# A two-layer SSM and SwiGLU kernel: another hand-written order ahead of the first feed-forward group, the norms' mean factor on GpSimd, and a float32 inverse for three more pairs

## The chip, the cores and the metric

The kernel runs on one core of a Trainium2 chip. The metric is the device time of one execution in microseconds (us). The core's engines are TensorE (PE in the profile; its weight loads are PEld), VectorE (DVE), ScalarE (ACT), GpSimd (POOL) and SyncE (SP, which here only issues DMAs). Each engine works through its own instructions strictly in the order in which they stand in the program; a semaphore makes an instruction wait for another engine or for a DMA, and everything behind it on that engine waits too.

## What is computed

Four steps on x of 2048 rows by 512 columns, float32; the two kinds of step use the same weights both times.

```python
def _A_ref(u, ...):                       # SSM as a long convolution, one filter per column
    P = exp((dt * A)[:, :, None] * arange(L));  K = einsum("dn,dnl,dn->dl", C, P, dt * B).real
    y = irfft(rfft(u, 2L) * rfft(K, 2L))[:L] + u * Dskip
def _B_ref(x, w_gate, w_up, w_down):      # feed-forward, F = 1376
    return (silu(x @ w_gate) * (x @ w_up)) @ w_down
x = x + _A_ref(layernorm(x)); x = x + _B_ref(layernorm(x))
x = x + _A_ref(layernorm(x)); x = x + _B_ref(layernorm(x))
```

## The kernel before

The 2048 rows are worked in four blocks of T = 512. With two layers this makes eight (layer, block) pairs, in the order `SEQ = ((0,0),(0,1),(0,2),(1,0),(0,3),(1,1),(1,2),(1,3))`. The text counts them from 1 to 8, so the third to fifth pair are (0,2), (1,0) and (0,3). Each pair goes through `ssm` and then `ffn`.

**Before the first pair**, eight channel chunks of 64 columns are turned into filters: `lags` forms the filter's lags on TensorE (tiles `pk`), `spectra`, `first_parts` and `later_parts` transform them (`pw`, `wo`, `wos`, `w0r`), and the results go to DRAM (`wdr`). In the same stretch the feed-forward weights are cut into two float16 halves: `split(h, l, n)` issues `n` loads of float32 columns or rows into staging tiles, makes `h` high halves and `l` low halves. High halves come from ScalarE (line 675; the very first one from VectorE, line 673; lines 700 for w_down), low halves from VectorE (680, 703). The staging tiles share their space with other tiles, so a load waits until those are free.

**`ssm_half(layer, b, h)`** takes one half of the columns (256) of one pair. Its four steps multiply the pair's spectrum by filter spectra on VectorE: line 812 writes `yk` or `t`, line 815 adds `t` into `yk`, 820 and 821 form the complex result. Pair (layer, b) needs b + 1 such products a step, with `w` and `uu` loaded from DRAM on the SP queue. Lines 767, 768 and 833 to 845 combine four results into the four operands `v` of the inverse transform, which `inverse` runs on TensorE into `pi` (line 784). `inverse` has two forms. For pairs whose index in `SEQ` is at least `INV` it makes a float16 high part (`yl`, ScalarE, 776) and a low part (`yl`, VectorE, 232 through `stt`), and TensorE runs six float16 products of 256 columns; for the others TensorE takes `v` itself in float32, two products, each two records in the profile. `result` adds `pi` to the residual (`xg`, `xf`). The constants of the float16 form, `eih`, lie in the place of the float32 form's `ei`, so that their load (line 745) waits for the last float32 inverse.

**Norms.** `row_stats` serves all norms but the first three: ScalarE makes the row sums and the sums of squares (223, 225, 226), GpSimd takes the power -1/2 into `rs` (227), and VectorE multiplies mean and `rs` into `nb` (228), after which ScalarE applies both. It runs 21 times, 15 times for two row groups and six times for four.

**`ffn(layer, b)`** works on two halves of 256 rows. Six groups `pgu` of 48 float16 products (930, 931, 933; 899 to 901 for the remainder of 96 columns) hold gate and up in PSUM, of which two are held at a time. ScalarE applies Silu (936), VectorE multiplies with up (937), ScalarE and VectorE make the halves `hh` and `hl` (938, 939), and 946 to 948 multiply them by w_down into `py`. So the third group can start only when the first one's line 937 is done.

**What sets the order.** Up to the first feed-forward group the order is written out by hand: inside `tc.manual_schedule` each engine's instructions stand as the code issues them. There `conv[0]` and `conv[1]` are the two column halves of the first pair's `ssm`, `tail["sp"]` is what is left of a chunk's `spectra`, `odd` and `rest` are `later_parts` of the last two chunks, `last` is one forward transform of the second block, `norm` the first feed-forward norm and `block1` the second pair's `ssm`; `take(x, n)` issues the next n pieces of x. Behind that section the compile step's scheduler merges what is issued; instructions under `tc.high_priority` go first.

Of the kernel before, what the change touches and what calls it, by code (L numbers as in the profile page):

```python
# [16 lines left out]
OP = mybir.AluOpType  # L17
# [58 lines left out]
def kernel(ctx, tc, x, a_re, a_im, b_re, b_im, c_re, c_im, log_dt, d_skip,  # L76
# [139 lines left out]
    def row_stats(src, rows, scale, tag, junk):  # L216

        mv = tl([P, 4, 2], "mv", tag)
        rs = tl([P, 8], "rs", tag)
        nb = rs[:, 4:]  # L220
        c = 1.0 / (math.sqrt(D) * scale)
        for r in range(rows):
            A.activation(junk(r), src[:, r], AF.Identity, scale=-c / D, accum_out=mv[:, r, 0:1])
        for r in range(rows):
            A.activation(junk(r), src[:, r], AF.Square, scale=c, bias=mv[:, r, 0:1], accum_out=mv[:, r, 1:2])
        A.activation(mv[:, :rows, 1], mv[:, :rows, 1], AF.Identity, bias=epst[:, 0:1] if scale == 1.0 else epst[:, 1:2])  # L226
        G.tensor_tensor(rs[:, :rows], mv[:, :rows, 1], mhalf[:, :rows], OP.pow)  # L227
        V.scalar_tensor_tensor(nb[:, :rows], mv[:, :rows, 0], 1.0 / c, rs[:, :rows], OP.mult, OP.mult)
        return rs, nb

    def stt(o, i0, s, i1, op1):
# [281 lines left out]
    def skip(ch, kt, eng):  # L513

        k = kt[0:1, :, 0]
        eng.tensor_tensor(k, k, dsk[:, ch * DC:(ch + 1) * DC].rearrange("p (g d) -> p g d", g=4), OP.add)
# [97 lines left out]
    def sizes(ch, kt, junk):  # L614

        A.activation(junk, kt, AF.Abs, accum_out=wsum[:, ch:ch + 1])
# [36 lines left out]
    def split_weights():  # L653
# [5 lines left out]
        def columns(j, wi, src):  # L659
            fs = slice(j * cb, (j + 1) * cb)  # L660
            sc = sc6[:, wi:wi + 1]
            at = []

            def load():
                tag = next(tags)
                st = tl([P, 4, cb], "st2", tag) if isinstance(tag, str) else \
                    wsl[3].bitcast(F32)[:, 4 * cb * tag:4 * cb * (tag + 1)].rearrange("p (k f) -> p k f", k=4)
                nc.sync.dma_start(st, src[:, fs].rearrange("(k p) f -> p k f", p=P))
                at.append(st)

            def hi():
                if j == 0 and wi == 0:
                    V.tensor_scalar(wgu(wi, 0, 0, 4)[:, :, fs], at[0], sc, None, OP.mult)
                else:
                    A.activation(wgu(wi, 0, 0, 4)[:, :, fs], at[0], AF.Copy, scale=sc)

            def lo():
                n = 2 if wi == 0 else 4
                for k in range(0, 4, n):
                    V.scalar_tensor_tensor(wgu(wi, k, 1, n)[:, :, fs], at[0][:, k:k + n], sc,  # L680
                                           wgu(wi, 0, 0, 4)[:, k:k + n, fs], OP.mult, OP.subtract)
            return load, hi, lo
# [292 lines left out]
    with tc.manual_schedule(engines={mybir.EngineType.Activation, mybir.EngineType.DVE, mybir.EngineType.PE, mybir.EngineType.Pool}):  # L975
# [228 lines left out]
        split(1, 0)  # L1204
        first_parts(c, 0)
        take(conv[0], 1)
        split(1, 1)
        split(0, 0, 1)
        first_parts(c, 2)
        split(1, 0)  # L1210
        take(conv[0], 1)
        first_parts(c - 1, 1)
        split(1, 0)
        take(last, 2)
        take(conv[1], 1)
        first_parts(c - 1, 3)
        take(conv[1], 1)
        split(0, 1)
        split(0, 0, 1)
        take(conv[0], 1)  # L1220
        take(conv[1], 1)
        split(1, 1)
        split(0, 0, 1)
        take(conv[1], 1)
        split(0, 1)
        split(0, 0, 1)
        take(odd, 2)
        take(conv[1], 1)
        direct_size()
        block1 = ssm(0, 1)  # L1230
        take(norm, 1)
        take(rest, 2)
        take(odd, 1)
        take(odd, 2)
        take(norm, 1)
        take(block1, 1)
        take(rest, 1)
        split(1, 0)
        take(odd, 1)
        take(norm, 1)  # L1240
        split(0, 1)
        take(rest, 3)
        take(conv[0], 1)
        take(conv[1], 1)
        ready = nhl2[:, 0, 0], nhl2[:, 0, 1]
        split(1, 1)
        take(rest, 3)
        split(1, 1)
        take(rest, 4)
        split(0, 0, 3)  # L1250
        sizes(c, kts[1], ks)
        nn2 = tl([P, 2, D], "nn2", "nn")
    small[0] = itertools.repeat("sml")
    pscale = product_scale()
# [52 lines left out]
```

## Time and profile before

| | |
|---|---|
| median of three runs | 1091.86 us (1090.23 to 1092.86) |
| the profiled execution | 1091.58 us, span 1089.4 us |
| TensorE busy | 1026.5 us, 94% of the span |
| VectorE busy | 969.3 us, 89% |
| ScalarE busy | 547.4 us, 50% |
| GpSimd busy | 109.6 us, 10% |
| first product of a feed-forward group | at 300.5 us |

The profile's stretches, rows by line and waits below are all from that one execution, in us from its start. "Busy" is time in which at least one of an engine's instructions ran; two neighbours on an engine overlap a little at their ends, so the distance from one start to the next is somewhat less than an instruction's duration, and on TensorE much less. A releaser behind "<-" names what ended a wait.

### The profile page before, as it was taken

The page shows a single profiled execution, that of the slowest core. Times are in us where ns is not written, and L with a number is a line of the kernel's source. Part 1 is how long each engine was busy: PE and PEld are TensorE (multiplying, and loading weights), DVE is VectorE, ACT ScalarE, POOL GpSimd, SP SyncE. Part 2 cuts the span into 40 slices and gives each one's busy share as a digit, 9 for nine tenths or more (in the row PEclk, how much of TensorE's full clock was granted, in tenths as well). Part 3 has the DMA queues.
Part 4 walks back from the last instruction along what each step waited for, and adds up shares of the span by engine and source line. Part 5 has one row for each costly group of instructions (what it writes and reads, how often), then busy time and mean ns, then how long its engine had stood idle before and what let it go on. Part 6 is the DMA issues. An engine that isn't in the chain of part 4 may idle for free.

```text
span 1089.4 us, 22811 instructions
## 1 busy us (share of the span) xinstructions
PE 1026.5 (94%) x9302; PEld 810.9 (74%) x9302; DVE 969.3 (89%) x1405; ACT 547.4 (50%) x1093; POOL 109.6 (10%) x163
## 2 busy tenths in 40 slices
PE   1989999998779999999999999999999999999998
PEld 1868888887677777686779676786867687686775
DVE  8999999998999999999999989999998999993221
ACT  6989998953367162466462253533425432134211
POOL 1112222220002010012010001201100000000000
PEclk9989999998989999999999999999999999999999
DMA  5366777768765356342444553443545245312000
GB/s 212 108 180 167 173 166 179 187 181 272 234 182 172 120 145 215 105 141 68 131 117 133 158 160 130 119 136 100 166 126 180 59 127 147 109 61 63 2 25 20
DMA packets 125003, 149.23 MB, mean 137 GB/s; under 512 B 50897, under 2 KB 75985, under 8 KB 124130
## 3 DMA queue, kind: packets, MB, share of 16 engines
q1 hardware_dynamic: 112994, 122.27, 36.8%
q0 software_dynamic: 11904, 25.50, 10.0%
q8 instruction: 73, 1.20, 0.5%
q14 instruction: 32, 0.26, 0.1%
HBM read 97.66 MB, written 33.82 MB: 121 GB/s over the span
## 4 chain that ended last, share of the span: by engine, by line
PE 27%; DVE 27%; issue 11%; DMA 5%; ACT 3%; POOL 1%; SPq 0%; DVEq 0%; POOLq 0%; ACTq 0%
PE pgu L930 5%; PE pgu L931 5%; PE pgu L933 5%; DVE t L812 4%; DVE yk L815 4%; PE py L948 3%; PE py L946 3%; PE py L947 3%; DVE yk L812 3%; PE pi L784 2%; DVE sg L937 2%; DVE hl L939 2%; DMA n<-xdr 1%; DVE yl L232 1%; DMA mix<-nn 1%
## 5 line engine op out<-in xcount | busy, mean ns | idle before, releaser
L930 PE MATMUL pgu<-mix,wsl 128*128 128x256 f16 x1280 | 298.6, 273 | 5.4 <-DVE sg L937 2.1
L931 PE MATMUL pgu<-mix,wsl 128*128 128x256 f16 x1280 | 298.4, 273 | 0.0
L933 PE MATMUL pgu<-mix,wsl 128*128 128x256 f16 x1280 | 194.8, 273 | 0.0
L931 PEld LDWEIGHTS <-wsl 128*128 128x128 f16 x1280 | 125.2, 98 | 22.5 <-issue 6.7
L933 PEld LDWEIGHTS <-wsl 128*128 128x128 f16 x1280 | 125.2, 98 | 18.4 <-issue 3.8
L930 PEld LDWEIGHTS <-wsl 128*128 128x128 f16 x1280 | 125.2, 98 | 16.4 <-issue 1.2
L946 PE MATMUL py<-wsl,hh 128*128 128x512 f16 (+1 forms) x352 | 134.2, 381 | 0.1
L948 PE MATMUL py<-wsl,hl 128*128 128x512 f16 (+1 forms) x352 | 133.5, 381 | 0.1
L947 PE MATMUL py<-wsl,hh 128*128 128x512 f16 x320 | 121.8, 381 | 0.0
L815 DVE TENSOR_TENSOR yk<-yk,t 128x1024 f32<-128x1024 f32 x96 | 116.9, 1218 | 0.5
L812 DVE TENSOR_TENSOR t<-uu,w 128x1024 f32<-128x1024 f32 x96 | 117.0, 1218 | 0.3
L938 ACT ACTIVATE hh<-sg 128x512 f16<-128x512 f32 x80 | 50.1, 627 | 114.0 <-DVE sg L937 114.0
L544 PE MATMUL pw<-kt,ek 128*128 128x256 f32 (+1 forms) x384 | 93.2, 381 | 0.0
L937 DVE SCALAR_TENSOR_TENSOR sg<-pgu,sc,sg 128x512 f32<-128x512 f32 x80 | 59.6, 745 | 37.7 <-ACT sg L936 37.6
L936 ACT ACTIVATE sg<-pgu,sc 128x512 f32<-128x512 f32 x80 | 54.2, 678 | 70.7 <-PE pgu L933 66.9
L544 PEld LDWEIGHTS pw<-kt,ek 128*128 128x128 f32 x384 | 74.8, 199 | 8.8
L939 DVE TENSOR_TENSOR hl<-sg,hh 128x512 f16<-128x512 f32 x80 | 54.8, 685 | 15.3 <-ACT hh L938 15.3
L227 POOL TENSOR_TENSOR rs<-mv,mhalf 128x2 f32<-128x2 f32 (+1 forms) x21 | 33.6, 1598 | 336.3 <-ACT mv L226 296.3
L509 PE MATMUL pk<-re,g 128*32 128x64 f32 x1024 | 65.0, 317 | 2.2 <-DMA g<-g 1.9
L948 PEld LDWEIGHTS <-hl 128*128 128x128 f16 (+1 forms) x352 | 34.4, 98 | 39.2 <-issue 0.8
L947 PEld LDWEIGHTS <-hh 128*128 128x128 f16 (+1 forms) x352 | 34.6, 98 | 38.4 <-issue 0.8
L510 PE MATMUL pk<-im,g 128*32 128x64 f32 x1024 | 63.1, 301 | 0.0
(265 smaller groups left out, 2010.1 us busy)
## 6 DMA issues: line engine op xcount, KB each, us to landing
uu<-udr SPq DMA_DIRECT2D x96, 256.0 KB, 3.0
w<-wdr SPq DMA_DIRECT2D x96, 256.0 KB, 2.8
g<-g POOLq DMA_DIRECT2D x6, 1024.0 KB, 9.2
udr<-fu POOLq DMA_DIRECT2D x22, 256.0 KB, 2.7
udr<-u SPq DMA_DIRECT2D x16, 256.0 KB, 3.3
n<-xdr SPq DMA_DIRECT2D x4, 1024.0 KB, 6.4
kdr<-ks SPq DMA_DIRECT2D x6, 512.0 KB, 2.9
kt<-kdr SPq DMA_DIRECT2D x24, 128.0 KB, 3.0
```

The source lines that it names most:

```text
L509: PE.matmul(o, lhsT=g[:, 0, :, d], rhs=re[:, 0:64, d], start=True, stop=False, tile_position=(0, 32 * grp))
L544: PE.matmul(pw[:, i], lhsT=e, rhs=kt[:, :, c + 4 * k0:4 * k1:4, :].rearrange("p g k d -> p k g d"), start=c == 0, stop=c == 3)
L812: V.tensor_tensor(t, uu.unsqueeze(2).to_broadcast([P, NQ, 2, 2, DC]), w.unsqueeze(3).to_broadcast([P, NQ, 2, 2, DC]), OP.mult)
L815: V.tensor_tensor(yk, yk, t, OP.add)
L930: PE.matmul(o, lhsT=wgu(wi, k, 0)[:, fs], rhs=nh[:, k], start=k == 0, stop=False)
L931: PE.matmul(o, lhsT=wgu(wi, k, 1)[:, fs], rhs=nh[:, k], start=False, stop=False)
L933: PE.matmul(o, lhsT=wgu(wi, k, 0)[:, fs], rhs=nlo[:, k], start=False, stop=k == 3)
L937: V.scalar_tensor_tensor(sg, pgu[:, 1], sc6[:, 4:5], sg, OP.mult, OP.mult)
L939: V.tensor_tensor(hl[:, f0:f0 + 2], sg, hh[:, f0:f0 + 2], OP.subtract)
L946: PE.matmul(py[r], lhsT=hh[:n, f, rc], rhs=wd(f, 0)[:n], start=f == 0, stop=False)
L947: PE.matmul(py[r], lhsT=hh[:n, f, rc], rhs=wd(f, 1)[:n], start=False, stop=False)
L948: PE.matmul(py[r], lhsT=hl[:n, f, rc], rhs=wd(f, 0)[:n], start=False, stop=f == FT - 1)
```

## The change

Three edits. `INV` goes from 2 to 5, so that the third to fifth pair take the float32 inverse. In `row_stats` the scale moves out of the sums and `nb` becomes one GpSimd multiplication. In the hand-written section many `take` and `split` calls stand in another order; one of them, `take(block1, 1)`, is gone, and the very first high half of the weights moves from VectorE to ScalarE.

```diff
-INV = 2
+INV = 5
...
-        c = 1.0 / (math.sqrt(D) * scale)
+        c = 1.0 / (D * scale ** 2)
...
-            A.activation(junk(r), src[:, r], AF.Identity, scale=-c / D, accum_out=mv[:, r, 0:1])
+            A.activation(junk(r), src[:, r], AF.Identity, scale=-1.0 / D, accum_out=mv[:, r, 0:1])
...
-            A.activation(junk(r), src[:, r], AF.Square, scale=c, bias=mv[:, r, 0:1], accum_out=mv[:, r, 1:2])
-        A.activation(mv[:, :rows, 1], mv[:, :rows, 1], AF.Identity, bias=epst[:, 0:1] if scale == 1.0 else epst[:, 1:2])
+            A.activation(junk(r), src[:, r], AF.Square, bias=mv[:, r, 0:1], accum_out=mv[:, r, 1:2])
+        A.activation(mv[:, :rows, 1], mv[:, :rows, 1], AF.Identity, scale=c,
+                     bias=epst[:, 0:1] if scale == 1.0 else epst[:, 1:2])
         G.tensor_tensor(rs[:, :rows], mv[:, :rows, 1], mhalf[:, :rows], OP.pow)
-        V.scalar_tensor_tensor(nb[:, :rows], mv[:, :rows, 0], 1.0 / c, rs[:, :rows], OP.mult, OP.mult)
+        G.tensor_tensor(nb[:, :rows], mv[:, :rows, 0], rs[:, :rows], OP.mult)
...
-                if j == 0 and wi == 0:
-                    V.tensor_scalar(wgu(wi, 0, 0, 4)[:, :, fs], at[0], sc, None, OP.mult)
-                else:
-                    A.activation(wgu(wi, 0, 0, 4)[:, :, fs], at[0], AF.Copy, scale=sc)
+                A.activation(wgu(wi, 0, 0, 4)[:, :, fs], at[0], AF.Copy, scale=sc)
...
         take(conv[0], 1)
-        take(tail["sp"], 2)
+        take(conv[0], 1)
         spread_pe(ks, kts[1])
         skip(c, kts[1], G)
+        take(tail["sp"], 2)
...
-        take(block1, 1)
...
```

What the new order means is seen in the instructions. The change shifts the line numbers: 812, 815, 871, 609, 703, 680, 833, 841, 232 and 784 of before are 810, 813, 869, 610, 701, 678, 831, 839, 233 and 782 in it.

The first place is VectorE behind the first feed-forward norm's mean factor (213), before:

```order
L213 SCALAR_TENSOR_TENSOR rs<-mv,rs 128x2
L609 TENSOR_TENSOR wos<-pw,wos 128x2x3x64
L812 TENSOR_TENSOR yk<-u,w0r 128x1024
L812 TENSOR_TENSOR t<-uu,w 128x1024
L815 TENSOR_TENSOR yk<-yk,t 128x1024
L703 SCALAR_TENSOR_TENSOR wsl_2663<-st_3002,sc_92,wsl_2663 128x512 x2
L820 TENSOR_TENSOR bb<-yk 128x256
L821 TENSOR_TENSOR bb<-yk 128x256
L812 TENSOR_TENSOR t<-uu,w 128x1024
L812 TENSOR_TENSOR yk<-u,w0r 128x1024
L815 TENSOR_TENSOR yk<-yk,t 128x1024
```

The same place in the change:

```order
L213 SCALAR_TENSOR_TENSOR rs<-mv,rs 128x2
L701 SCALAR_TENSOR_TENSOR wsl_2663<-st_2935,sc_92,wsl_2663 128x512 x2
L610 TENSOR_TENSOR wos<-pw,wos 128x2x3x64
L869 TENSOR_TENSOR mix<-pt,mix 128x1024
L678 SCALAR_TENSOR_TENSOR wsl_2661<-wsl_2664,sc_92,wsl_2661 128x2x344
L678 SCALAR_TENSOR_TENSOR wsl_2662<-wsl_2664,sc_92,wsl_2661 128x2x344
L610 TENSOR_TENSOR wos<-pw,wos 128x2x3x64
```

The second pair's products (812, 815, 820, 821 from `u`, `uu` and `w`) have left this place; the low half of the first norm's output (869) and the weights' low halves stand directly behind the norm. Counted from the first pair's first product to the first line 937, VectorE has 118 instructions before and 96 in the change: four `t`, four `yk` from `u`, three of 815, four each of 820 and 821, two of 767, one of 768 and the 673 are fewer, and one 623 (a scalar of the inverse's scale) is added.

The second place is the inverse of the third pair's first column half. On VectorE, before:

```order
L833 TENSOR_TENSOR bb<-bb,mix 128x512
L815 TENSOR_TENSOR yk<-yk,t 128x1024
L910 TENSOR_TENSOR sg_3034<-sg_3034 128x2x96
L836 TENSOR_TENSOR mix<-bb 128x256
L837 TENSOR_TENSOR mix<-bb 128x256
L841 TENSOR_TENSOR bb<-bb,mix 128x512
L232 SCALAR_TENSOR_TENSOR yl_4065<-bb,sy,yl_4065 128x512
```

and in the change:

```order
L831 TENSOR_TENSOR bb<-bb,mix 128x512
L937 TENSOR_TENSOR hl<-sg_3021,hh 128x512
L813 TENSOR_TENSOR yk<-yk,t 128x1024
L233 SCALAR_TENSOR_TENSOR z_3022<-n,z_3022 128x1024
L834 TENSOR_TENSOR mix<-bb 128x256
L835 TENSOR_TENSOR mix<-bb 128x256
L839 TENSOR_TENSOR bb<-bb,mix 128x512
```

The low part `yl` is gone there, with its partner on ScalarE. On TensorE the same inverses are, in the change, products straight from `bb`:

```order
L782 MATMUL pi<-bb,mix 128x256 x2
L944 LDWEIGHTS hh
L944 MATMUL py<-wsl_2663,hh 128x512
L782 MATMUL pi<-bb,mix 128x256 x2
L945 LDWEIGHTS hh
```

where before six rows of the form `pi<-yl_4065,mix` stood for each operand.

The third place is GpSimd. Each power is now followed by the factor (229):

```order
L228 TENSOR_TENSOR rs<-mv,mhalf 128x2
L229 TENSOR_TENSOR rs<-mv,rs 128x2
L228 TENSOR_TENSOR rs<-mv,mhalf 128x4
L229 TENSOR_TENSOR rs<-mv,rs 128x4
L904 MEMSET sg_3021 128x4x32 x2
L737 DMA udr_114<-fu 128x512 x2
```

Behind these on GpSimd's queue stand the stores of a block's spectra (737), as before. On the SP queue the load of `eih` (745 before) moves from the third pair's start to the sixth's.

More of the change, by code (lines that the diff above doesn't have):

```diff
@@ L1203 @@
         scales()
-        split(1, 0)
+        take(conv[0], 1)
         first_parts(c, 0)
-        take(conv[0], 1)
-        split(1, 1)
-        split(0, 0, 1)
         first_parts(c, 2)
         split(1, 0)
+        first_parts(c - 1, 1)
+        first_parts(c - 1, 3)
+        take(conv[1], 1)
         take(conv[0], 1)
-        first_parts(c - 1, 1)
+        take(conv[1], 1)
+        split(0, 1)
+        split(0, 0, 1)
+        take(conv[1], 1)
         split(1, 0)
@@ L1215 @@
         take(conv[1], 1)
-        first_parts(c - 1, 3)
+        split(1, 0)
         take(conv[1], 1)
+        take(norm, 1)
+        split(0, 0, 1)
+        take(odd, 2)
+        take(rest, 2)
+        take(norm, 1)
+        split(1, 0)
+        take(odd, 1)
+        take(norm, 1)
+        ready = nhl2[:, 0, 0], nhl2[:, 0, 1]
+        block1 = ssm(0, 1)
         split(0, 1)
         split(0, 0, 1)
[L1220 to L1224, printed above, removed]
+        take(rest, 1)
         split(0, 1)
```

26 lines of the change are left out of this document (10 added, 16 removed).

## The prediction, made before the changed kernel ran

> **What bounds the kernel now.** I read the page's head, then busy time by stretch, then what TensorE waited for, then single rows. Of the page:
>
> ```profile
> PE 1026.5 (94%) x9302; PEld 810.9 (74%) x9302; DVE 969.3 (89%) x1405; ACT 547.4 (50%) x1093; POOL 109.6 (10%) x163
> ```
>
> The stretches (start and end, length, then busy us and instructions of TensorE, its weight loads, VectorE, ScalarE, GpSimd; granted clock, DMA share, GB/s):
>
> ```profile
> 246.00:300.00 54.00, 44.95 (x469) 39.78 (x468) 48.74 (x85) 17.84 (x28) 1.89 (x2) 0.91 0.79 256
> 300.00:329.00 29.00, 20.97 (x147) 19.31 (x147) 27.94 (x38) 19.76 (x47) 0.00 (x0) 0.88 0.61 182
> 329.00:420.00 91.00, 91.00 (x765) 68.67 (x763) 89.79 (x145) 40.99 (x80) 15.35 (x15) 1.00 0.53 152
> 420.00:700.00 280.00, 272.00 (x2272) 209.11 (x2270) 270.46 (x404) 133.34 (x265) 21.87 (x28) 0.99 0.43 132
> 700.00:910.00 210.00, 205.51 (x1686) 153.85 (x1684) 200.37 (x292) 83.73 (x160) 15.28 (x21) 1.00 0.45 130
> 910.00:1089.00 179.00, 175.20 (x1465) 132.38 (x1461) 94.52 (x134) 46.54 (x82) 2.00 (x5) 1.00 0.18 54
> ```
>
> There are two regimes. Up to 329 us VectorE is nearly full (27.94 of 29) while TensorE is idle for 8 of 29. From 329 us on TensorE is full: 743.7 of 760 us. So the end is the time at which TensorE becomes dense, plus its work from there, plus its waits. The last column of numbers on VectorE, 94.52 of 179, says that VectorE finishes early and doesn't set the end.
>
> What TensorE waited for, from 256 to 329 us and from 329 us on (total, times, longest):
>
> ```profile
> PE pw L544 <- DVE wos L609: 7.4, 2, 5.7
> PE pi L784 <- DVE bb L833: 3.6, 1, 3.6
> ...
> PE pi L784 <- ACT yl L776: 5.8, 4, 2.0
> PE pf L277 <- ACT fbt L278: 2.5, 1, 2.5
> PE pgu L930 <- DVE sg L937: 2.1, 2, 1.6
> ```
>
> All waits in the early stretch end on VectorE, which has the second pair's products between those that TensorE needs. The longest later wait is the float16 inverse's for its high part.
>
> **Part 1, the order up to the first gate product.** Two groups of the first feed-forward half can run before line 937 of the first is done; the third is where TensorE becomes dense:
>
> ```profile
> 292.34 0.15 DVE L213 SCALAR_TENSOR_TENSOR rs<-mv,rs 128x2 f32<-128x2 f32 x1
> ...
> 327.95 0.75 DVE L937 SCALAR_TENSOR_TENSOR sg<-pgu,sc,sg 128x512 f32<-128x512 f32 x1
> ...
> 328.75 0.27 PE L930 MATMUL pgu<-mix,wsl 128*128 128x256 f16 x1 [1.90 <-DVE sy L623]
> ```
>
> By the order, TensorE has the same things behind it at that point before and after: both column halves of the first pair, all of `later_parts`, 96 products of the group. So whatever the first 937 gains, the end gains, as far as TensorE stays dense. VectorE's rows up to there:
>
> ```profile
> L680 DVE SCALAR_TENSOR_TENSOR wsl<-wsl,sc,wsl 128x1376 f16<-128x1376 f32 (+1 forms) x8 | 10.1, 1285 | 0.0
> L812 DVE TENSOR_TENSOR yk<-u,w0r 128x1024 f32<-128x1024 f32 x5 | 6.1, 1217 | 0.0
> L815 DVE TENSOR_TENSOR yk<-yk,t 128x1024 f32<-128x1024 f32 x4 | 4.9, 1222 | 0.1
> L820 DVE TENSOR_TENSOR bb<-yk 128x256 f32<-128x256 f32 x10 | 4.3, 425 | 0.3
> L680 DVE SCALAR_TENSOR_TENSOR wsl<-st,sc,wsl 128x688 f16<-128x688 f32 x4 | 3.5, 927 | 0.0
> L703 DVE SCALAR_TENSOR_TENSOR wsl<-st,sc,wsl 128x512 f16<-128x512 f32 x4 | 2.8, 746 | 0.9 <-ACT wsl L700 0.9
> L609 DVE TENSOR_TENSOR wos<-pw,wos 128x384 f32<-128x384 f32 x4 | 2.2, 552 | 1.0 <-ACT wos L608 1.0
> L572 DVE TENSOR_TENSOR wo<-pw,wo 128x768 f32<-128x768 f32 x1 | 1.0, 969 | 2.3 <-ACT w0r L568 2.3
> L673 DVE TENSOR_SCALAR wsl<-st,sc 128x1376 f16<-128x1376 f32 x1 | 0.9, 936 | 0.0
> ```
>
> Ahead of 213 the change takes away 673 (0.9), one wide 680 (1.6, from the first row less its four narrow ones), four narrow ones (3.7), and a reduction left out of the sum; it adds one `yk` (1.2). The wait of 2.3 at 572 goes, because a step of the first pair now stands ahead of it. That is 5.0 + 2.3, so 213 falls to about 285. From 213 to 937 the change has 28 instructions where before had 44: six narrow and three wide 680 (10.4), four 703 (3.0), six 609 (3.3), one `t` and one 815 (2.4), one 871 (taken as an 815, 1.2), two 793 and a reduction (2, estimate from the 703) and scalars, about 23. Without any wait the first 937 would stand at 308, 20 us earlier. It will wait, since the cover is gone: the w_down load can only start when the first pair's last inverse frees its place, and it took this long:
>
> ```profile
> 291.33 5.25 DMA st<-in_B_w_down_dram
> ```
>
> VectorE's 703 stands right behind 213 now and needs that load and ScalarE's high half (0.7 by the 703's like); ScalarE then has 869, a wide high half and four pieces of `wos` ahead of the first 609. I count 2.5 to 3 us of waiting at each of these two and 1 at the next wide low half and at the Silu, 7 in all: the first 937 at 315, a gain of 13. The bounds are 20 (no wait) and 8 (the waits nearly double).
>
> **Part 2, the inverse.** One inverse in float32 (four records) and in float16 (six), each with the instruction that follows:
>
> ```profile
> 332.68 1.03 PE L784 MATMUL pi<-mix 128*128 128x256 f32 x4
> 333.54 0.27 PE L930 MATMUL pgu<-mix,wsl 128*128 128x256 f16 x1
> ...
> 550.26 0.82 PE L784 MATMUL pi<-yl,mix 128*128 128x256 f16 x6
> 550.91 0.82 PE L277 MATMUL pf<-z,eh 128*128 128x256 f16 x6
> ```
>
> From start to start that is 0.86 against 0.65 us. Three pairs with eight inverses each are 24 × 0.21 = 5.0 us more work on the engine that is full, with nothing to hide it. What it takes away lies on the other two:
>
> ```profile
> L776 ACT ACTIVATE yl<-bb,sy 128x512 f16<-128x512 f32 x32 | 22.8, 716 | 24.5 <-DVE bb L833 12.2 <-PE pi L784 8.0 <-DVE bb L837 4.2
> L232 DVE SCALAR_TENSOR_TENSOR yl<-bb,sy,yl 128x512 f16<-128x512 f32 x32 | 23.8, 745 | 1.1 <-ACT yl L776 1.1
> ```
>
> That is 24 × 0.72 = 17 us of ScalarE and 24 × 0.75 = 18 us of VectorE. Neither is full where TensorE is dense at the end, so their busy time is worth nothing by itself; what counts is the wait of 5.8 us for `yl` quoted above. It can go to zero (the second pair's float32 inverses lie in 329 to 420, where TensorE is busy for 91.00 of 91) or come back as a wait for `bb`, as 3.6 did before 329. I take 5 of it as gone. The load of `eih` moves to the sixth pair, where it waits for the last float32 inverse as it did at the third; the filter loads queue behind it on SP for as long. I cost it at nothing, and cover is VectorE's loaded `w` and `uu`; if that is gone, one landing of some 3 us.
>
> **Part 3, the mean factor.** VectorE loses the first of these rows, GpSimd gains one of its own:
>
> ```profile
> L228 DVE SCALAR_TENSOR_TENSOR rs<-mv,rs 128x2 f32<-128x2 f32 (+1 forms) x21 | 3.3, 157 | 10.4 <-POOL rs L227 10.4
> L227 POOL TENSOR_TENSOR rs<-mv,mhalf 128x2 f32<-128x2 f32 (+1 forms) x21 | 33.6, 1598 | 336.3 <-ACT mv L226 296.3 <-DVE sg L937 31.7 <-DMA uu<-udr 8.2
> L516 DVE TENSOR_TENSOR kt<-kt,tdk x7: 204/206/207, 73.0 to 239.0; 1x64 f32<-1x64 f32 x7
> L516 POOL TENSOR_TENSOR kt<-kt,tdk x1: 553/553/553, 261.3 to 261.3; 1x64 f32<-1x64 f32 x1
> ```
>
> VectorE is rid of 3.3 us of work and 10.4 of standing behind the power. GpSimd's price isn't in the trace: 0.4 us by the addition that ran on both engines (2.7 times VectorE's 0.157), 1.6 by the power. Its nearest kin is the plain addition, so 0.4 to 0.6. The chain from `rs` to the normed rows grows by 0.3 to 1.4 us, 21 times; behind the factor on GpSimd queue only the spectra's stores, behind ScalarE's waiting instruction the Silus. The chain is covered as long as a pair's last result comes well before the next feed-forward half. On TensorE I cost this part at nothing, between a gain of 2 (the wait for `sg`) and a loss of 21 × 1.4 = 29 if nothing covered it.
>
> The Trainium skill speaks against this part: "GPSIMD Engine Reference", section 4.1, gives elementwise two-input work on a tile to VectorE, since GpSimd takes about twice as long for it. The trace agrees in direction (0.553 against 0.206 for one addition). Followed to the letter the rule would make this a loss; that case is the third rival.
>
> **What the moved work does afterwards.** About 18 us of the second pair's products (four `t`, four `yk`, three 815, eight pieces like 820, three sums) now stand behind the first 937. VectorE has to fit them into a stretch in which it is busy for 89.79 of 91 us. Two rows say how much room there is:
>
> ```profile
> L793 DVE TENSOR_TENSOR xg<-xg,pi x4: 681/682/684, 342.1 to 384.6; 128x512 f32<-128x512 f32 x4
> ...
> L953 DVE SCALAR_TENSOR_TENSOR xg<-py,sc,xg x2: 745/746/746, 416.2 to 418.7; 128x512 f32<-128x512 f32 x2
> ```
>
> The second pair's last result came at 384.6, the first pair's last feed-forward result at 416.2: 31 us ahead. With 18 more the second pair is still 13 us early, and the 18 us that part 2 takes off come back over the following pairs. But between the second and third gate product there are now some 9 us of VectorE's work against 48 × 0.109 = 5.2 us of TensorE's, and TensorE no longer has inverses to fill in. I charge 2 us.
>
> **The sum**, against the profiled execution's 1091.58 us (2.2 more than the span, 0.3 under the median): − 13 for the order, + 5 for the float32 products, − 5 for the wait on `yl`, + 2 for the debt, 0 for the mean factor: 1080.6, say 1081.
>
> **Rivals.**
> 1. The debt decides. If VectorE's 18 us delay the second pair beyond the end of the first pair's feed-forward, TensorE pays for them again: 1081 + 18 = 1099. It decides once the second pair's results come less than a norm's length before the first pair's last `py`; for it speaks VectorE's 89.79 of 91, against it the 31 us.
> 2. The order gains only 8, and the waits for `yl` come back as waits for `bb`: 1091.6 − 8 + 5 + 2 = 1090.6, no change. For it speaks that load, ScalarE's queue and VectorE now wait in turn; against it, that VectorE's 18 us are really gone from the path.
> 3. GpSimd's factor delays Silus: with 0.9 us at each of 21 norms, 1081 + 19 = 1100. Against it: ScalarE already waited for 228 and TensorE waited only 2.1 us for `sg`.
> 4. More than forecast: no wait ahead of the first 937 and no early debt, 1091.6 − 20 + 5 − 6 = 1070.6.
>
> **Chances.** Forecast 0.66 (its own range 1074 to 1088), rivals 0.11, 0.13, 0.04 and 0.06. The range 1072 to 1092 takes in the forecast and nearly all of rival 2, and leaves out most of 1, 3 and 4. A change under 0.2%, about 2 us, can't be told from none here. Faster by more: 0.66 + 0.06 + a third of rival 2, 0.77. Slower by more: 0.11 + 0.04 + a fifth of rival 2, 0.17; the same: 0.06.
>
> **What would show it.** The first 937 at 310 to 320 us and the first float16 group product ten or more us ahead of 300; no wait of TensorE for `yl` between the third and fifth pair; TensorE's inverses of those pairs at 0.86 us; no rows of VectorE waiting for the power; TensorE's waits from the first 937 on not above 20 us. It would be wrong if VectorE's `sg` became TensorE's main releaser in the first feed-forward, or if the first 937 waited for weight loads up to 320.

## The result and the profile after

The changed kernel takes 1098.1 us (median of 12 runs, 1092.5 to 1103.0) against 1091.8 us before (12 runs, 1089.3 to 1092.9): ratio 1.0052, 95% interval 1.0032 to 1.0072. It is slower, by half a per cent; the forecast was 1081, with 1072 to 1092 as its range. The profiled execution took 1094.0 us, span 1092.2, so it is one of the quicker ones: 4 us of the median aren't in it. A second profile, of a run of 1096.9 us, shows the same waits, somewhat longer.

The head of the page, then the stretches (start and end, length, then busy us and instructions of TensorE, its weight loads, VectorE, ScalarE, GpSimd; granted clock, DMA share, GB/s):

```profile
PE 1029.6 (94%) x9254; PEld 811.6 (74%) x9254; DVE 950.2 (87%) x1359; ACT 533.2 (49%) x1070; POOL 116.9 (11%) x184
```

```profile
246.00:300.00 54.00, 42.75 (x468) 37.45 (x467) 41.60 (x77) 20.09 (x33) 2.65 (x2) 0.88 0.65 207
300.00:329.00 29.00, 27.74 (x216) 24.88 (x215) 25.35 (x35) 22.86 (x51) 1.63 (x2) 0.98 0.77 245
329.00:420.00 91.00, 88.25 (x722) 65.65 (x720) 87.06 (x134) 35.87 (x71) 9.88 (x14) 0.98 0.46 127
420.00:700.00 280.00, 270.31 (x2165) 207.17 (x2164) 265.06 (x388) 118.46 (x244) 32.93 (x42) 0.99 0.49 143
700.00:910.00 210.00, 206.77 (x1703) 155.80 (x1702) 193.63 (x276) 84.07 (x157) 14.64 (x26) 1.00 0.42 124
910.00:1092.00 182.00, 177.82 (x1476) 133.48 (x1474) 99.99 (x141) 46.65 (x82) 2.40 (x7) 1.00 0.19 59
```

TensorE's rise comes sooner (27.74 of 29 us busy from 300 to 329, where it was 20.97), but it is no longer dense behind it: 88.25 of 91 us and 270.31 of 280, where it was 91.00 and 272.00. What it waited for, from 420 us on (total, times, longest):

```profile
PE pf L278 <- ACT fu L279: 6.5, 1, 6.5
PE pgu L928 <- DVE sg L935: 2.6, 4, 1.5
PE pf L278 <- ACT z L268: 1.2, 1, 1.2
PE pi L782 <- DVE bb L831: 0.9, 1, 0.9
...
PE pi L782 <- ACT yl L774: 0.4, 1, 0.4
```

The wait for `yl` is gone, 5.8 to 0.4 us. In its place stands one wait that the kernel before did not have, 6.5 us for ScalarE's eviction `fu` of the next forward transform.

One number used below is worked out from all of TensorE's rows: for each product the distance to the next one's start beyond the median distance of its kind, summed from 256 us on. The medians are taken over all the kernels of this document, and the sums are good to about 1 us. This lost time was 44.4 us before (27.2 of it by 329 us) and 42.5 in the change (19.6 by 329 us); in its second profile 45.3. The plain work in the same stretch was 783.3 and 788.0 us. So in the profiled runs 7.6 us were won by 329 us, the float32 products took 4.7 back, and 5.7 us were lost again behind 329 us.

VectorE's way to the first gate product, with what it waited for (start, length, instruction, in brackets the idle time ahead and what ended it):

```profile
264.70 1.22 DVE L810 TENSOR_TENSOR yk<-mix,w0r 128x1024 f32<-128x1024 f32 x1 [3.46 <-ACT w0r L591]
...
282.21 0.43 DVE L834 TENSOR_TENSOR bb<-bb 128x256 f32<-128x256 f32 x1 [1.31 <-PE pi L782]
283.06 0.42 DVE L835 TENSOR_TENSOR bb<-bb 128x256 f32<-128x256 f32 x1 [0.43 <-PE pi L782]
...
289.47 0.16 DVE L213 SCALAR_TENSOR_TENSOR rs<-mv,rs 128x2 f32<-128x2 f32 x1 [0.61 <-POOL rs L210]
292.11 1.41 DVE L701 SCALAR_TENSOR_TENSOR wsl<-st,sc,wsl 128x512 f16<-128x512 f32 x2 [2.48 <-ACT wsl L698]
296.55 0.56 DVE L610 TENSOR_TENSOR wos<-pw,wos 128x384 f32<-128x384 f32 x1 [3.03 <-ACT wos L609]
...
306.83 0.56 DVE L610 TENSOR_TENSOR mix<-pw,mix 128x384 f32<-128x384 f32 x1 [2.72 <-ACT mix L609]
...
319.67 0.75 DVE L935 SCALAR_TENSOR_TENSOR sg<-pgu,sc,sg 128x512 f32<-128x512 f32 x1 [0.16 <-ACT sg L934]
```

The gate product stands at 319.67, 8.3 us earlier than before and 4.7 later than forecast. The first product of a feed-forward group came at 294.25, 6 us ahead of 300.5, where the prediction asked for ten or more.

### The profile page after: what moved, and what is told of

Read it like the earlier page. It is cut to its first block, busy times and chain, and to the rows that moved or that the text cites. A ratio compares the mean times of both kernels' runs of the same rounds, so it can differ in the third digit from the quotient of the medians.

```text
span 1092.2 us, 22669 instructions
## 1 busy us (share of the span) xinstructions
PE 1029.6 (94%) x9254; PEld 811.6 (74%) x9254; DVE 950.2 (87%) x1359; ACT 533.2 (49%) x1070; POOL 116.9 (11%) x184
## 4 chain that ended last, share of the span: by engine, by line
PE 29%; DVE 26%; ACT 8%; DMA 6%; issue 4%; POOL 2%; SPq 0%; DVEq 0%; ACTq 0%; POOLq 0%
DVE t L810 5%; PE pgu L931 5%; PE pgu L928 5%; PE pgu L929 5%; DVE yk L813 4%; PE py L944 3%; PE py L945 3%; PE py L946 3%; DVE yk L810 3%; DMA n<-xdr 2%; PE pi L782 2%; DVE sg L935 2%; DMA mix<-nn 2%; DVE hl L937 2%; ACT junk L225 1%
## 5 line engine op out<-in xcount | busy, mean ns | idle before, releaser
L929 PE MATMUL pgu<-mix,wsl 128*128 128x256 f16 x1280 | 300.5, 274 | 0.0
L944 PEld LDWEIGHTS <-hh 128*128 128x128 f16 (+1 forms) x352 | 34.4, 98 | 37.8 <-ACT hh L936 0.5
L945 PEld LDWEIGHTS <-hh 128*128 128x128 f16 (+1 forms) x352 | 34.4, 98 | 36.7
```

What stands on the lines that cost most here:

```text
L929: PE.matmul(o, lhsT=wgu(wi, k, 1)[:, fs], rhs=nh[:, k], start=False, stop=False)
L944: PE.matmul(py[r], lhsT=hh[:n, f, rc], rhs=wd(f, 0)[:n], start=f == 0, stop=False)
L945: PE.matmul(py[r], lhsT=hh[:n, f, rc], rhs=wd(f, 1)[:n], start=False, stop=False)
```

## The experiments

All times are medians, the ratios those to the kernel before on the same chip, with 95% intervals. The kernel before took 1091.6 to 1093.0 us beside them. A difference between kernels of different rounds is one of medians from different chips; taken from the ratios it comes out up to 1.6 us otherwise.

**First round: which of the three parts.** Theory A: GpSimd's mean factor takes back what the order gains. Theory B: the second pair's products that now stand later come back as waits. Theory C: the float32 inverses cost their work and more. Each kernel is the one before with a part of the change's diff: order_only the new `take` and `split` calls with the first high half by ScalarE, norm_only the lines of `row_stats`, inverse_only and (with order_only's lines) order_inverse this one:

```diff
-INV = 2
+INV = 5
```

> The new order alone; INV stays 2 and the mean factor stays on VectorE. Theory A (the order gains what the first gate product of the change showed, 327.95 to 319.67, and GpSimd's mean factor takes it back): 1091.8 - 8 = 1084, between 1081 and 1087, first line 937 at about 320, and VectorE's multiplication with up waits on TensorE's path as little as before. Theory B (the debt: the second pair's products that now stand behind the first gate product come back as waits of TensorE in the first two pairs): 1090 to 1094, with the first feed-forward results early and the lead gone by the end of the second pair. Theory C (the float32 inverses are what costs): as A, 1084.

> INV = 5 alone; order and norms as before. TensorE's work grows by 5.0 us (1026.5 busy before). Theory A: the wait of 5.8 us for yl goes with it, 1090 to 1093, no change. Theory C (the float32 form costs its work and the waits only change their name): 1091.8 + 5 = 1097, up to 1099. Theory B says nothing of it: 1092 to 1097.

> Only the norms: the scale leaves the sums and the mean factor is one GpSimd multiplication (21 times, 0.2 to 2.1 us each in the change's trace). Theory A: ScalarE stands behind GpSimd for some 38 us in all instead of 17, its Silus and feed-forward pieces come late, TensorE waits 6 to 9 us more: 1098 to 1101. Theories B and C: the chain is covered, and VectorE is rid of 3.3 us and of 10.4 us of standing: 1090 to 1092.

> The new order with INV = 5, the mean factor on VectorE as before. Theory A: the change without its harmful part, 1084 to 1088, at least 8 us under the change's 1098. Theory B: 1093 to 1098. Theory C: 1084 + 5 = 1089 to 1092, and the rest of the change's 1098 spread over all three parts.

| | us | ratio |
|---|---|---|
| order_only | 1087.95 | 0.9966 (0.9955 to 0.9978) |
| inverse_only | 1094.61 | 1.0033 (1.0017 to 1.0049) |
| norm_only | 1106.09 | 1.0131 (1.0109 to 1.0154) |
| order_inverse | 1085.88 | 0.9947 (0.9930 to 0.9964) |

The norm's edit costs 14.5 us by itself and 12.2 on top of the other two. The other two together gain 5.7. Theory A is right that the loss comes with the norm's edit, and C falls: it had forecast 1089 to 1092 for order_inverse. B holds in part: order_only was 6.7 us ahead by 329 us (lost time 20.5 against 27.2) and then lost 8.3 us between 470 and 520, where the kernel before lost 1.6 and order_inverse 0.1. The stretch from 420 to 520 of order_only, then of order_inverse:

```profile
420.00:520.00 100.00, 94.18 (x772) 70.99 (x770) 96.92 (x149) 52.12 (x105) 9.72 (x14) 0.98 0.49 142
```

```profile
420.00:520.00 100.00, 100.00 (x801) 76.85 (x799) 97.76 (x156) 49.30 (x102) 11.28 (x17) 1.00 0.50 143
```

VectorE is nearly full in both, and TensorE is full only where VectorE is rid of the third pair's `yl` pieces. By these figures order and inverse belong together: -3.7 and +3.0 alone, -5.7 as a pair.

**Second round: why the norm's edit costs.** Theory D: GpSimd's short multiplication can't start beside VectorE's instructions with two SBUF inputs, and ScalarE stands behind it. Theory E: it is the scale's move or the rest of the rewriting. Theory F: ScalarE has the norm's apply too soon in its order, wherever the factor runs. The edits are to the changed kernel:

```diff
-        G.tensor_tensor(nb[:, :rows], mv[:, :rows, 0], rs[:, :rows], OP.mult)
# factor_vector
+        V.tensor_tensor(nb[:, :rows], mv[:, :rows, 0], rs[:, :rows], OP.mult)
# factor_scalar
+        for r in range(rows):
+            A.activation(nb[:, r:r + 1], mv[:, r, 0:1], AF.Identity, scale=rs[:, r:r + 1])
```

In factor_twice the removed line stands twice; port_alone is a kernel of its own, as its expectation tells.

> The changed kernel with one engine exchanged: the mean factor is the same multiplication, but on VectorE; the scale stays out of the sums. Theory D (GpSimd's short instruction cannot start while VectorE's instructions with two SBUF inputs follow one another, 0.20 us when VectorE is idle and up to 2.1 us in the change, 6.8 us with the norm's edit alone, and ScalarE stands behind it): back to the version with order and inverse alone, 1084 to 1088. Theory E (the scale's move or the plan that the compile step makes of the rewritten norm costs the 12 us): stays at 1095 to 1100.

> The changed kernel with the mean factor's multiplication issued twice in a row on GpSimd, same result (21 more GpSimd instructions). Theory D: the second one waits for VectorE like the first, ScalarE stands 10 to 20 us longer in all, and the time grows again by something like the first one's 12 us: 1104 to 1112. Theory E: 21 times 0.2 to 0.4 us, partly covered, 1098 to 1102.

> The changed kernel with the mean factor on ScalarE: two or four small instructions a norm (54 in all, 0.2 to 0.3 us each by the small ScalarE instructions of the norms, 11 to 16 us of ScalarE's work). It shares no port with VectorE, and VectorE no longer stands behind the power. Theory D: 1082 to 1088, as good as on VectorE or better. Theory F (what costs is that ScalarE has the apply directly behind the power in its order, wherever the factor runs): 1092 to 1098.

> The disputed cost by itself; the kernel leaves the whole computation out. Six stretches: three powers and three multiplications of 128x2 on GpSimd while VectorE is idle, or works off ten instructions of 128x512 float32 in a row: two SBUF inputs; one SBUF and one PSUM input; scalar_tensor_tensor with two SBUF inputs; tensor_scalar with one SBUF input; three with two SBUF inputs and one with PSUM by turns. Theory D: idle and the PSUM stretch alike, 0.70 and 0.20 us; with two SBUF inputs no GpSimd instruction ends before VectorE's ten are done (some 7 us); by turns one GpSimd instruction per PSUM instruction. Theory E: GpSimd's instructions take the same time in all stretches, or at most one VectorE instruction (0.7 us) more.

factor_vector took 1087.32 (0.9944, 0.9922 to 0.9966), within its interval the same as order_inverse: no cost of the scale's move shows, and E falls. factor_twice took 1108.02 (1.0141, 1.0114 to 1.0167), which D had forecast. But factor_scalar took 1097.91 (1.0047, 1.0031 to 1.0064), as much as the change, with no GpSimd multiplication at all: D as the whole cause falls, and F stands. This run has a weakness: the factor on ScalarE is 54 instructions with 12.4 us of ScalarE's own work, which may cost something too. port_alone gave GpSimd's prices (power L71, multiplication L72; first beside VectorE's ten instructions with two SBUF inputs, then beside ten with one SBUF and one PSUM input):

```profile
20.80 1.07 POOL L71 TENSOR_TENSOR rs<-go,mh 128x2 f32<-128x2 f32 x1 [1.29 <-ACT go L69]
21.95 0.63 POOL L72 TENSOR_TENSOR rs<-mv,rs 128x2 f32<-128x2 f32 x1
...
27.48 0.69 POOL L71 TENSOR_TENSOR rs<-go,mh 128x2 f32<-128x2 f32 x1 [1.28 <-ACT go L69]
28.25 0.19 POOL L72 TENSOR_TENSOR rs<-mv,rs 128x2 f32<-128x2 f32 x1
```

```profile
20.04 6.10 DVE L44 TENSOR_TENSOR o<-xa 128x512 f32<-128x512 f32 x10
...
26.73 6.06 DVE L48 TENSOR_TENSOR o<-xa,pt 128x512 f32<-128x512 f32 x10
```

Beside two SBUF inputs the multiplication takes 0.63 instead of 0.19 us, some part of one VectorE instruction more; it did not have to wait for all ten, so D's strong form was wrong too. That is real, and 21 × 0.44 makes 9 us; how much of it reaches TensorE depends on what stands behind the apply.

**What ScalarE's order shows.** ScalarE from the third pair's second feed-forward norm on, in the changed kernel, and GpSimd beside it:

```profile
510.34 0.30 ACT L226 ACTIVATE mv<-mv,epst 128x2 f32<-128x2 f32 x1
514.86 0.81 ACT L881 ACTIVATE nn<-xf,rs 128x512 f32<-128x512 f32 x1 [4.22 <-POOL rs L229]
515.70 0.63 ACT L882 ACTIVATE nn<-nn 128x512 f16<-128x512 f32 x1
517.09 0.81 ACT L881 ACTIVATE nn<-xf,rs 128x512 f32<-128x512 f32 x1 [0.76 <-DVE nn L883]
521.71 0.63 ACT L882 ACTIVATE nn<-nn 128x512 f16<-128x512 f32 x1 [3.80 <-DMA mix<-nn]
522.24 0.58 ACT L279 ACTIVATE fu<-pf 128x512 f32<-128x512 f32 x1
```

```profile
510.77 2.61 POOL L228 TENSOR_TENSOR rs<-mv,mhalf 128x2 f32<-128x2 f32 x1 [11.17 <-ACT mv L226]
513.46 1.36 POOL L229 TENSOR_TENSOR rs<-mv,rs 128x2 f32<-128x2 f32 x1
```

The same place in order_inverse:

```profile
509.92 0.30 ACT L226 ACTIVATE mv<-mv,epst 128x2 f32<-128x2 f32 x1
514.57 0.60 ACT L278 ACTIVATE fu<-pf 128x512 f32<-128x512 f32 x1 [4.35 <-PE pf L277]
515.06 0.80 ACT L880 ACTIVATE nn<-xf,rs 128x512 f32<-128x512 f32 x1
```

Here is the 6.5 us wait. `fu` could run at about 514.5 in both, when the six products into `pf` were done. In the change it stands behind both applies, the second of which also waits 3.80 us for a transposing DMA to free `nn`, and comes at 522.24. The wait has a second cost, in the clock that TensorE was granted (columns as in the stretches above). The same 6.4 us in the change and then in order_inverse:

```profile
520.00:526.40 6.40, 3.53 (x17) 2.46 (x17) 4.60 (x9) 1.79 (x4) 0.00 (x0) 0.50 0.74 148
```

```profile
520.00:526.40 6.40, 6.40 (x61) 5.74 (x59) 3.23 (x6) 2.86 (x4) 0.00 (x0) 1.00 0.74 200
```

At 0.50 the gate products behind the wait stand 0.21 us apart instead of 0.11, which makes 1.7 us of lost time more.

Against order_inverse the norms did not become longer: from the last sum to the first apply the 21 norms took 50.2 us in all in the change and 55.4 in order_inverse. What changed is what ScalarE does meanwhile. The static order is the order of an engine's instructions that the compile step fixes. Between the sums' last instruction and the first apply ScalarE's static order has 16 other instructions in the change and 31 in order_inverse, most of them `sg`, `hh`, `fbt` and `fu`, which TensorE needs soon. In the change they stand behind the apply, and ScalarE stands ahead of it (ScalarE's waits for `rs`, before, in order_inverse and in the change):

```profile
ACT nn L883 <- DVE rs L228: 15.8, 11, 3.2
ACT n L255 <- DVE rs L228: 1.0, 2, 0.7
```

```profile
ACT nn L880 <- DVE rs L228: 17.6, 11, 2.5
ACT n L255 <- DVE rs L228: 4.7, 4, 2.2
```

```profile
ACT nn L881 <- POOL rs L229: 24.9, 14, 4.2
ACT n L256 <- POOL rs L229: 13.2, 6, 3.3
```

That is 16.8 us before, 22.3 in order_inverse and 38.1 in the change. The traces hold only a part of the 12.2 us, since the change's profiled runs were among its quicker ones and order_inverse's among its slower: the spans differ by 5.4 and 8.3 us.

**Third round: the place in the order against the engine.** If the place decides, a longer chain should help: one more VectorE instruction behind the factor makes the compile step put the apply later. Theory G: any new plan is a throw of the dice.

It is added behind the factor in the change (factor_touch), order_inverse (vector_touch), norm_only (norm_touch) and factor_scalar (scalar_touch); order_norm_touch is factor_touch with INV = 2, and touch_third has the line only for the feed-forward norms of (0, 2):

```diff
+        V.tensor_scalar(nb[:, :rows], nb[:, :rows], 1.0, None, OP.mult)
```

The second edit moves a piece of the weights ahead of VectorE's first wait, in order_inverse (order_filled), factor_touch (touch_filled) and the change (change_filled):

```diff
         take(conv[0], 1)
+        split(1, 0)
         first_parts(c, 0)
         first_parts(c, 2)
-        split(1, 0)
         first_parts(c - 1, 1)
         first_parts(c - 1, 3)
+        split(0, 1)
         take(conv[1], 1)
         take(conv[0], 1)
         take(conv[1], 1)
-        split(0, 1)
```

> The changed kernel, its mean factor multiplied on GpSimd as in the change, and then once more by 1.0 on VectorE, so that the apply waits for both: a longer chain with the same GpSimd work. In the static order of ScalarE, 34 other instructions then stand between the 21 norms' sums and their first apply; 31 stand there with order and inverse alone (1085.9 us), 16 in the change (1098.1), 21 with the factor on ScalarE (1097.9). Theory F (what costs is that ScalarE reaches the apply too soon in its order and stands there, with the Silus and the transforms' evictions behind it): 1084 to 1090 in spite of the longer chain. Theory D (GpSimd's multiplication itself is the cost): 1098 to 1104.

> Order and inverse alone (the mean factor on VectorE as before), with one more VectorE multiplication by 1.0 behind each mean factor: 21 more VectorE instructions of 0.15 us in the chain, and 44 instead of 31 other ScalarE instructions ahead of the applies. Theory F: 1083 to 1088, no slower than without it. Theory D, or any in which the norm's length decides: 21 times 0.2 to 0.5 us more, 1088 to 1094.

> The changed kernel once more for a second profile: its runs spread over 10 us (1092.5 to 1103.0), and the first profile showed a run of 1094.0. Theory F: the same places wait (the third pair's transform behind ScalarE's apply, the multiplication with up), longer where GpSimd's power and factor are longer; 1095 to 1100.

> Order and inverse alone, with one piece of the weights (a high half on ScalarE, its low half on VectorE, 1.8 us) moved ahead of the first pair's second column half, where VectorE stood 3.45 us for the filter spectra w0r. By the step of the prediction that counted only 7 of some 15 us of such waiting, the first gate product comes 1.5 to 2 us earlier and the end with it: 1083 to 1085. If other waits take it up (the weights' loads behind the norm, 3.7 us): 1085 to 1087.

> The changed kernel with the extra VectorE multiplication by 1.0 at two of the 21 norms only, the feed-forward norms of the third pair. In ScalarE's order the eviction fu (line 279) of the next transform now stands ahead of that norm's second apply instead of behind it; in the change TensorE waited 6.5 and 6.8 us for it. Theory F: that one wait falls to 1 us or less and the time by 5 to 6 us, 1091 to 1094. Theory G (every plan is a throw of the dice, one wait less here is one more elsewhere): 1095 to 1101.

> The norm's edit alone on the old order and INV = 2 (1106.1 us), with the extra VectorE multiplication by 1.0 behind GpSimd's mean factor at all 21 norms; ScalarE has 33 instead of 23 other instructions ahead of the applies (28 in the kernel before). Theory F: the 14.5 us are gone, 1088 to 1094. Theory D (GpSimd's multiplication costs by itself): 1104 to 1110.

> factor_touch (1082.5 us) with INV = 2 again: order and norm with the extra multiplication, the float16 inverse for the third to fifth pair. TensorE has 5.0 us less work. By the prediction's part 2 (5 us of work against 5 us of waits for yl): 1081 to 1084. If the waits for yl stay small without the norm's trouble: 1078 to 1080. If the float16 form's VectorE work is what TensorE waits for: 1085 to 1088.

> factor_touch (1082.5 us) with the piece of the weights moved ahead of VectorE's 3.45 us wait for w0r, as in order_filled, where TensorE had lost 2.3 us less by 329 us but the end came no earlier. Theory F: the early gain stays where the later waits are short: 1080 to 1082. Theory G: 1082 to 1090.

> The changed kernel with the piece of the weights moved as in order_filled, and nothing else. ScalarE then has 18 other instructions ahead of the norms' applies (16 in the change; 32 and 34 in the two filled versions with VectorE in the chain, 1089.9 and 1093.7 us). Theory F: still a short-chain plan, 1095 to 1105. Theory G (any new plan is a throw of the dice around the same mean): as likely under 1092 as over 1096.

> factor_scalar (mean factor on ScalarE, 1097.9 us) with the extra VectorE multiplication by 1.0 behind it; 37 instead of 21 other ScalarE instructions ahead of the applies. Theory F: 1084 to 1092, whichever engine makes the factor. Theory G: 1086 to 1100.

after_again took 1096.9 us, with 6.8 us of waiting for `fu` and 5.2 for `sg` (line 935) from 329 us on, 6.5 and 5.2 in the first profile. The others:

"Others" is the number of other ScalarE instructions ahead of the 21 first applies in the static order; "lost" is TensorE's lost time from 256 us on in the profiled run. Counted in the traces instead (ScalarE's instructions between line 226 and the norm's first apply, without the norms' own) the numbers come out within three of these; the same count gives 33 for factor_vector, 35 for order_only and 36 for inverse_only.

| kernel | others | us | ratio | lost |
|---|---|---|---|---|
| the change | 16 | 1098.12 | 1.0052 (1.0032 to 1.0072) | 42.5 |
| touch_third | 16 | 1095.14 | 1.0019 (1.0004 to 1.0034) | 46.3 |
| factor_twice | 18 | 1108.02 | 1.0141 (1.0114 to 1.0167) | 59.1 |
| change_filled | 18 | 1113.04 | 1.0197 (1.0179 to 1.0214) | 58.1 |
| factor_scalar | 21 | 1097.91 | 1.0047 (1.0031 to 1.0064) | 43.9 |
| norm_only | 23 | 1106.09 | 1.0131 (1.0109 to 1.0154) | 62.3 |
| before | 28 | 1091.8 | 1 | 44.4 |
| order_inverse | 31 | 1085.88 | 0.9947 (0.9930 to 0.9964) | 37.1 |
| order_filled | 32 | 1089.87 | 0.9969 (0.9951 to 0.9987) | 37.4 |
| order_norm_touch | 32 | 1095.22 | 1.0033 (1.0020 to 1.0047) | 47.7 |
| norm_touch | 33 | 1092.76 | 1.0005 (0.9993 to 1.0018) | 41.6 |
| touch_filled | 34 | 1093.70 | 1.0011 (0.9994 to 1.0028) | 41.8 |
| factor_touch | 34 | 1082.51 | 0.9915 (0.9899 to 0.9932) | 31.5 |
| scalar_touch | 37 | 1090.82 | 0.9981 (0.9967 to 0.9994) | 39.3 |
| vector_touch | 44 | 1097.50 | 1.0052 (1.0033 to 1.0070) | 47.7 |

One needless VectorE instruction takes 15.6 us off the change, 13.3 off norm_only and 7.1 off factor_scalar, with GpSimd's multiplication still in the first two. The multiplication got shorter by it, from 16.4 to 11.1 us in all in the change and from 25.9 to 8.5 in norm_only. But the norms did not: from last sum to first apply they took 50.2 us and then 64.3, 61.8 and then 61.1, and 45.8 and then 76.1 without any GpSimd multiplication (factor_scalar and scalar_touch). So a longer chain came with the shorter time. GpSimd's price can still count where little stands ahead of the apply: factor_twice has 67.4 us there and took 9.9 us more than the change. factor_touch is the fastest kernel of all, 9 us under the one before; from 420 us on TensorE waits for little there:

```profile
PE pgu L929 <- DVE sg L936: 1.2, 3, 0.7
PE pi L783 <- DVE bb L832: 0.8, 1, 0.8
PE pgu L929 <- DVE sg L907: 0.8, 2, 0.4
```

vector_touch goes against theory F, which had forecast 1083 to 1088. The chain leads through VectorE twice there, and TensorE waits (from 329 us on) for the normed rows themselves:

```profile
PE pgu L899 <- DMA mix<-nn: 11.9, 2, 9.0
```

Both waits belong to the norm at 402 us, where no other ScalarE instruction stands ahead of the apply, neither here nor in order_inverse. What came late was behind it: VectorE made the last low half at 415.9 us instead of 410.6, its transposing DMA was issued at 417.3 instead of 411.4, by then behind the stores and loads of x, and it landed 9.3 us later, where the median of these was 3.2. So the place in ScalarE's order isn't the only one that counts, and no best place is shown. What is shown is that the plans in which little stands ahead of the applies, 16 to 23 others, are all slower than the kernel before. change_filled, one more plan with the short chain, was the slowest of all, above the 1095 to 1105 that theory F gave it; what rose there most (from 329 us on) was again what ScalarE feeds:

```profile
PE pgu L928 <- DVE sg L935: 10.7, 8, 2.5
PE pf L278 <- ACT z L268: 4.4, 2, 2.7
```

Theory G is not out. touch_third removed the wait for `fu` (no such row is left) and gained 3.0 us, not 5 to 6; in its profiled run, its slowest with 1097.4 us, TensorE waited 8.2 us for `sg` (5.2 in the change, from 329 us on) and 3.1 for `xg` (0.5). order_filled and touch_filled lost less by 329 us (19.2 and 20.5 against 21.5 and 22.2) and ended 4 and 11 us later than without it; for touch_filled that is above both theories' forecasts (1082 and 1090 at most). With 28 to 37 others ahead the times still run from 1082.5 to 1095.2, and order_norm_touch, at the upper end and above all that was forecast for it (1088 at most), lost 11.2 us between 470 and 520; order_only, also with INV = 2, had lost 8.3 there.

## Why the prediction was wrong

**Part 3, the mean factor "at nothing" on TensorE: this step failed.** It cost 12.2 us on top of the other parts. The price of the instruction was somewhat above the forecast of 0.4 to 0.6, with a mean of 0.78, 16.4 us in all instead of 8 to 13:

```profile
L229 POOL TENSOR_TENSOR rs<-mv,rs 128x2 f32<-128x2 f32 (+1 forms) x21 | 16.4, 781 | 1.5
```

What failed is the sentence on the cover, "the chain is covered as long as a pair's last result comes well before the next feed-forward half". It asked whether the normed rows come in time, and they did: no wait of TensorE for a DMA of `mix` from `nn` is in the change's rows from 329 us on. It named the Silus behind ScalarE's waiting instruction, but did not ask how many other instructions would still stand ahead of the apply. The static order of ScalarE, readable beforehand, had dropped from 28 other instructions ahead of the applies to 16. Rival 3 had the right place: ScalarE's wait for `rs` rose by 21.3 us, and its 21 × 0.9 was 19. That its 1100 lies near 1098 is partly luck: the part cost 12.2, not 19, on top of a kernel that took 1085.9, not 1081, and a lengthened chain was not the reason, since factor_touch has the longer one. It got a chance of 0.04, on the argument that TensorE had waited only 2.1 us for `sg`: a figure from the old order, which the change removed. Its label was half wrong, since the factor on ScalarE costs the same. The Trainium skill's rule beside it ("GPSIMD Engine Reference", section 4.1, elementwise work to VectorE) had the sign of the outcome; by the runs it was not the reason, since the fastest kernel has the multiplication on GpSimd.

**Part 1, the order, 13 us.** This term was mis-sized. The first gate product came 8.3 us earlier in the change's profiled run, at the lower bound of 8, and 7.2 and 6.4 earlier in order_only and order_inverse, below it. Line 213 stood at 289.5 where the sum had 285. The waits behind the norm came as counted (2.48 and 3.03 us against 2.5 to 3 each). Missing from the sum were 3.46 us ahead of the norm, where `yk` waits for `w0r`, 1.74 us in two waits for `pi`, and a second wait of 2.72 at a 610: some 15 us instead of 7. order_filled moved work into the first of these and TensorE lost 2.3 us less by 329 us, so that wait was real; what it gave did not reach the end, for a reason that stays open.

**Part 2, the inverse, +5 and -5.** Both terms were right: TensorE's work grew by 4.8 us (order_inverse 788.1 against 783.3) and the wait for `yl` fell from 5.8 to 0.4. It did not come back as a wait for `bb`, as rival 2 had it: that is 1.1 us from 329 us on. Alone the edit came out at +3.0 us, and in inverse_only's trace the wait changed its name, 1.4 us for `yl` but 7.5 for `sg` where it had been 2.1. On top of the order it came out at -2.1; that it takes from VectorE what the order loads onto it fits the two stretches above.

**The debt, 2 us.** With the inverse it was covered (lost time between 470 and 520: 0.1 in order_inverse). Without, order_only paid 6.7 us more there than the kernel before. Rival 1's own condition was not met in either: the second pair's last result came at 401.4 us in the change and 400.1 in order_only, some 11 us ahead of the first pair's last `py` in both (13 forecast). If what order_only lost is the debt, it was paid a pair later.

Without part 3 the forecast of 1081 would have met 1085.9 to 1087.3, 5 to 6 us off, nearly all of it the mis-sized first term (13 against 8.3).

What stays open: how the 12.2 us divide between the place in the order, GpSimd's longer instructions and the chance of a new plan; why plans with 28 to 37 others ahead still differ by 13 us; and why the change's runs spread over 10 us, where the twelve of the kernel before spread over 4 (over 7 to 9 in the larger sets beside the experiments). GpSimd's multiplication at an unchanged order was not tried, since the compile step plans anew for every edit.

## What to carry to other kernels

When an edit shortens a dependency chain by taking an engine out of it, look at what the scheduler then puts where on the engines at its ends: an in-order engine that reaches a waiting instruction sooner holds up everything behind it. Count what stands between producer and consumer in the static order before and after; here 31 to 16 came with 12 us more, and one useless instruction that put it back to 34 with 15.6 less. The count is a warning and not a price: at 32 to 34 others the times still ran from 1082.5 to 1095.2. With such a planner an edit's own price can be smaller than the new plan it brings, as it was here, so one build of each is not enough to judge the edit.

## What the runs showed of the hardware

GpSimd's instruction on 128x2 is stretched by VectorE's instructions beside it, by what these read: in port_alone the multiplication took 0.19 us beside one SBUF and one PSUM input, as with VectorE idle, and 0.63 beside two SBUF inputs. VectorE's ten instructions took 6.06 and 6.10 us, so no loss of VectorE's shows. The Trainium skill, "SBUF — State Buffer", section "Who interferes with whom", says that a VectorE instruction with two SBUF inputs contends with a GpSimd instruction that reads SBUF; the trace agrees, with 0.63 against 0.19 us. In norm_only, though, one multiplication lasted far longer than a VectorE instruction. GpSimd, then the first and the last VectorE instructions that lie within it, and the one behind:

```profile
333.88 6.82 POOL L229 TENSOR_TENSOR rs<-mv,rs 128x4 f32<-128x4 f32 x1
```

```profile
333.91 0.41 DVE L838 TENSOR_TENSOR bb<-bb 128x256 f32<-128x256 f32 x1
...
340.24 0.40 DVE L846 TENSOR_TENSOR bb<-bb 128x256 f32<-128x256 f32 x1
340.57 0.67 DVE L794 TENSOR_TENSOR xg<-xg,pi 128x512 f32<-128x512 f32 x1
```

Twelve VectorE instructions stand there one behind the other, none with a PSUM input, and it ends as the first that reads PSUM (`pi`) starts. In port_alone a GpSimd instruction got through within about one VectorE instruction. What tells the two apart was not found.

TensorE's granted clock stood at 0.50 behind two of its long waits: from 520 to 526.4 us in the change, behind the 6.5 us for `fu`, and from 415 to 432 us in vector_touch, around the 9.0 us for the normed rows.
